# An expert's 64-token tile in a bank of the first product's ring, and two opening loads issued by other engines

## The chip, the cores and the metric

The kernel runs on one core of one Trainium2 chip. The metric is device time in microseconds (us), of which the span of a profiled execution is nearly all. The engines are TensorE (PE, its weight loads PEld), VectorE (DVE), ScalarE (ACT), GpSimd (POOL) and SyncE (SP); DMAs are issued by SP, and before the change by GpSimd only where rows are gathered or scattered.

## The reference

Three stages follow each other on 4608 tokens of 512 channels:

```python
scores = scale * np.matmul(q, k.transpose(0, 1, 3, 2))        # 8 batches, 8 heads, 576 x 64
attn = np.matmul(scores * Dmat, v)                            # decay mask gamma^(i-j), i >= j
y = (((x @ w1) * (x @ w2)) @ w3) @ w_out                      # 512 -> 1024 -> 1024 -> 512
logits = y @ w_gate                                           # 8 experts
assigned = greedy by sorted logits, 576 tokens per expert
out[mask] = np.maximum(y[mask] @ e_w1[e], 0.0) @ e_w2[e]      # for each expert e
```

The weights of the middle stage come as 64-bit floats. Products are made in single precision by three products of halves: each operand is split into a high and a low part.

## The kernel before, in words

**Opening.** The list ORDER (line 23) sets the order in which SP issues the first loads: "q0 c0 k0 v0 c1 q1 k1 w0 v1 w1 ...": queries, keys and values of 128-token tile 0, 1, 2, constants c, and pairs of weight blocks w of 1 MB. Lines 1133 to 1142 walk the list and call `att_load` (line 238), which has an argument for the issuing engine that is SP by default. q and k of a tile are two DMAs each, v is one; their pieces are 64 floats, 256 bytes (128 rows by 8 heads for a tile). Two small buffers are cleared by GpSimd behind the loads, and SP then loads the router's weights (lines 1143 to 1145).

Attention of tile 0 runs through `att_scale` (line 261, VectorE scales q and k), `att_T` (274 to 276, transposes and a ScalarE copy), `att_P` (300, the first product that reads v and k), `att_QK` (283), `att_mask` (288), `att_state` (312). Beside it, `conv` (185 to 216) turns 64-bit weights into single-precision high and low parts: one ScalarE operation (196), four on VectorE (197 to 202), a copy and a subtraction (215, 216). The first weight products are at line 549.

**Experts.** `expert(e)` (line 1014) takes 576 tokens. Its first product (line 1027) is made in two halves of 256 and 320 tokens, for 8 blocks f of the hidden channels: 12 matmuls each into a PSUM bank that goes round a ring of four, HB = PX + PYb (line 982). PX are two tiles of one bank each (p2, p3; the profile calls them p); PYb are the two banks of one tile, PY (the profile's py). ScalarE (1036) and VectorE (1037) empty each bank into the operands `ht`; the second half is emptied in two pieces, of 256 and 64 columns.

The second product (line 1049) makes five output tiles o: four of 128 tokens (24 matmuls each), and tile 4 of 64 tokens (16 matmuls, for which the high and low operands lie side by side). Each takes a bank from `mm_bank()` (line 130), which alternates between the two banks MM. A tile is emptied by ScalarE (1055), tile 4 by ScalarE and a VectorE add (1058, 1059), into `osb`, two buffers in turn (1052), and GpSimd scatters it to the output rows (1060). Experts 0 to 6 write the tiles in the order 0, 1, 2, 3, 4, expert 7 in the order 0, 4, 1, 2, 3.

The order of instructions on each engine is fixed when the program is built, from dependencies and a timeline of the builder's own; the experts' part stands in a block of its own for that (line 1166). Side by side with an expert, the next one's weights are split (940, 941) and its tokens gathered (990), transposed (1005) and split (1010, 1011).

Of the kernel before, what the change touches and what calls it, by code (L numbers as in the profile page):

```python
# [84 lines left out]
def build(ctx, tc, io):  # L85
    nc = tc.nc
    PE, V, A, G, SP = nc.tensor, nc.vector, nc.scalar, nc.gpsimd, nc.sync
# [42 lines left out]
    def mm_bank():  # L130
        return MM[nxt("mm", 2)]

    def nxt(name, n):
        i = rot[name]
        rot[name] = (i + 1) % n
        return i
# [6 lines left out]
    def slot(i, k):  # L143
        if WS[i] is None:
            WS[i] = region(f"ws{i}", 4096, F32R)
        if (i, k) not in views:
            views[i, k] = WS[i].rearrange("p (k f) -> p k f", k=k)
        return views[i, k]
# [15 lines left out]
    def load_pair(n):  # L164

        t = RO[n // 2 % 2][:, 2048 * (n % 2):2048 * (n % 2) + 2048]
        i, w = n // 2, ("w1", "w2")[n % 2]
        for x in range(2):
            raws[w, 2 * i + x, 0] = t.bitcast(I32).rearrange("p (k x f c) -> p k x f c", k=4, x=2, c=2)[:, :, x]
        SP.dma_start(t.bitcast(mybir.dt.int64).rearrange("p (k f) -> p k f", k=4),  # L170
                     w64[w].rearrange("(k p) f -> p k f", k=4)[:, :, 256 * i:256 * i + 256])
# [47 lines left out]
    qkv = [[A0[:, 1024 * j + 512 * i:1024 * j + 512 * i + 512] for j in range(3)] for i in range(2)]  # L219
# [4 lines left out]
    def buf(t):  # L224

        b = qkv[t if t < 3 else (t + 1) % 2]
        return b[0], qkv[t % 3][1], b[2]
# [10 lines left out]
    def att_load(t, which=(0, 1, 2), eng=SP):  # L238
        for i in which:
            if t >= NT or (t, i) in loaded:  # L240
                continue
            loaded.add((t, i))
            x, src = buf(t)[i], (q, k, v)[i]
            p = 0
            while p < 128:
                b, s = divmod(128 * t + p, S)
                n = min(128 - p, S - s)
                if i == 2:
                    eng.dma_start(x[p:p + n].rearrange("p (h d) -> p h d", h=H),
                                 src[b, :, s:s + n, :].rearrange("h s d -> s h d"))  # L250
                else:
                    for r in range(2):
                        eng.dma_start(x[p:p + n].rearrange("p (c r d) -> p r c d", c=4, r=2)[:, r],
                                     src[b, 4 * r:4 * r + 4, s:s + n, :].rearrange("h s d -> s h d"))
                p += n
# [715 lines left out]
    def hT():  # L971

        if not hts:
            r = [region(f"g{j}", 3072, F32R) for j in range(3)] + [region("h3", 512, F32R)]
            for f in range(6):
                b = 1152 * (f % 2)
                hts.append((r[f // 2][:, b:b + 512], r[f // 2][:, b + 512:b + 1024], r[f // 2][:, b + 1024:b + 1152]))
            hts.append((r[0][:, 2304:2816], r[1][:, 2304:2816], r[0][:, 2816:2944]))
            hts.append((r[2][:, 2304:2816], r[3][:, 0:512], r[1][:, 2816:2944]))
        return hts  # L980

    HB = PX + PYb
# [31 lines left out]
    def expert(e):  # L1014
        wh, wl = (slot(i, 4) for i in pairs[(2 * e) % 3])
        yh = [h[:, k] for _, h, _ in yts[e % 2] for k in range(h.shape[1])]
        yl = [l[:, k] for _, _, l in yts[e % 2] for k in range(l.shape[1])]
        ht = hT()
        for half in range(2):
            ts = (slice(0, 256), slice(256, 576))[half]  # L1020
            n = ts.stop - ts.start
            for f in range(8):
                fs = slice(128 * f, 128 * f + 128)
                p = HB[nxt("hb", 4)]
                for kk in range(4):
                    for j, (w, x) in enumerate(((wh, yh), (wh, yl), (wl, yh))):
                        PE.matmul(p[:, :n], w[:, kk, fs], x[kk][:, ts], start=(kk == 0 and j == 0),  # L1027
                                  stop=(kk == 3 and j == 2))
                hh, hl, hr = ht[f]
                if half:  # L1030
                    parts = ((p[:, 0:256], hh[:, 256:512], hl[:, 256:512]),
                             (p[:, 256:320], hr[:, 0:64], hr[:, 64:128]))
                else:
                    parts = ((p[:, 0:256], hh[:, 0:256], hl[:, 0:256]),)
                for src, h, l in parts:
                    A.activation(h, src, AF.Relu)  # L1036
                    V.scalar_tensor_tensor(l, src, 0.0, h.bitcast(F32), op0=OP.max, op1=OP.subtract)  # L1037
                yield 1500
        vh, vl = (slot(i, 8) for i in pairs[(2 * e + 1) % 3])
        for o in (0, 1, 2, 3, 4) if e < E - 1 else (0, 4, 1, 2, 3):  # L1040
            p = mm_bank()
            for f in range(8):
                if o < 4:
                    s = slice(128 * o, 128 * o + 128)
                    ops = ((ht[f][0][:, s], vh), (ht[f][0][:, s], vl), (ht[f][1][:, s], vh))
                else:
                    ops = ((ht[f][2], vh), (ht[f][2], vl))
                for j, (x, w) in enumerate(ops):
                    PE.matmul(p, x, w[:, f, :], start=(f == 0 and j == 0), stop=(f == 7 and j == len(ops) - 1))  # L1049
                if f % 2:  # L1050
                    yield 1300
            ob = osb[nxt("osb", 2)]
            n = 128
            if o < 4:
                A.activation(ob, p, AF.Copy)  # L1055
            else:
                n = 64
                A.activation(ob[:64], p[64:128], AF.Copy)
                V.tensor_tensor(ob[:64], p[:64], ob[:64], op=OP.add)  # L1059
            st = G.indirect_dma_start(out=out, out_offset=bass.IndirectOffsetOnAxis(ap=idx[:n, 5 * e + o:5 * e + o + 1], axis=0),  # L1060
                                      in_=ob[:n], in_offset=None)
            for x in scat:
                tc.declare_no_dep(st.ins, x.ins, reason="rows of other tokens")
            scat.append(st)
# [68 lines left out]
    for c in ORDER.split():  # L1133
        n = int(c[1:])
        if c[0] == "c":
            a, b = (0, 272, 400, CST.shape[1])[n:n + 2]
            SP.dma_start(cst[:, a:b], io["cst"][:, a:b])
        elif c[0] == "w":
            load_pair(n)
            nload[0] = n + 1  # L1140
        else:
            att_load(n, ("qkv".index(c[0]),))
    G.memset(wg, 0.0)
    SP.dma_start(wg[:, :, 0:8], io["wgate"].rearrange("(c p) e -> p c e", p=128))
    G.memset(WG, 0.0)
# [20 lines left out]
    with tc.block(schedule_with_timeline_sim=True):  # L1166
        begin = tokens(0)
        drain(take_from(begin, 2))
        for e in range(E):
            def side(e=e):  # L1170
                if e + 1 < E:
                    yield from weights(e + 1, 1, V)
                    yield from tokens(e + 1)
            s = side()
            m = expert(e)
            if e == 0:
                drain(take_from(m, 3))
                drain(begin)
                drain(take_from(m, 3))
                drain(weights(0, 1, V))  # L1180
                drain(weights(1, 0, V))
                drain(take_from(m, 10))
            else:
                drain(take_from(m, 16))
            merge(m, s, 1.2)
            drain(s)
            if e + 2 < E:
                drain(weights(e + 2, 0, V))
# [28 lines left out]
```

## Time and profile before

| | |
|---|---|
| median of 3 runs | 1303.81 us (1303.66 to 1306.4) |
| profiled execution, its own time | 1303.38 us |
| its span | 1301.6 us |
| TensorE busy | 1256.4 us, 97% |
| VectorE, ScalarE, GpSimd busy | 41%, 35%, 20% |
| mean granted TensorE clock | 0.984 of full |

The span is what the profiler saw from the first to the last instruction; the execution's own time holds 1.78 us more. Busy times are sums over instructions. A bracket behind a row of the timeline gives the idle time of the engine ahead of it and what ended it.

### The profile page before, as it was taken

The page shows a single profiled execution, that of the slowest core. Times are in us where ns is not written, and L with a number is a line of the kernel's source. Part 1 is how long each engine was busy: PE and PEld are TensorE (multiplying, and loading weights), DVE is VectorE, ACT ScalarE, POOL GpSimd, SP SyncE. Part 2 cuts the span into 40 slices and gives each one's busy share as a digit, 9 for nine tenths or more (in the row PEclk, how much of TensorE's full clock was granted, in tenths as well). Part 3 has the DMA queues.
Part 4 walks back from the last instruction along what each step waited for, and adds up shares of the span by engine and source line. Part 5 has one row for each costly group of instructions (what it writes and reads, how often), then busy time and mean ns, then how long its engine had stood idle before and what let it go on. Part 6 is the DMA issues. An engine that isn't in the chain of part 4 may idle for free. (4 is left out here: it accounts for less than half of the span.)

```text
span 1301.6 us, 27200 instructions
## 1 busy us (share of the span) xinstructions
PE 1256.4 (97%) x11416; PEld 1112.1 (85%) x11416; DVE 529.0 (41%) x1298; ACT 460.8 (35%) x989; POOL 254.4 (20%) x238
## 2 busy tenths in 40 slices
PE   5789999999999999999999999989999999999996
PEld 4678988889898989889899777778989989899885
DVE  6797544433231312212212555553533524335220
ACT  4443433343322222212221544333543534435221
POOL 1101211112211120201110734432120211211011
PEclk7799999999999999999999999999999999999999
DMA  9766444422312131424012312163533524435110
GB/s 243 221 163 198 133 131 134 127 64 61 83 34 74 25 83 25 131 87 134 10 49 93 114 45 98 42 190 119 154 121 114 157 67 150 140 96 153 47 39 29
DMA packets 156382, 136.00 MB, mean 104 GB/s; under 512 B 119264, under 2 KB 119520, under 8 KB 155232
## 3 DMA queue, kind: packets, MB, share of 16 engines
q1 hardware_dynamic: 150368, 115.35, 30.3%
q0 software_dynamic: 5888, 18.88, 4.6%
q8 instruction: 91, 1.49, 0.5%
q14 instruction: 35, 0.29, 0.1%
HBM read 107.19 MB, written 27.00 MB: 103 GB/s over the span
## 5 line engine op out<-in xcount | busy, mean ns | idle before, releaser
L549 PE MATMUL p<-x,ws 128*128 128x384 f32 x2304 | 424.1, 339 | 1.7 <-POOL x L345 0.9
L549 PEld LDWEIGHTS p<-x,ws 128*128 128x128 f32 x2304 | 398.2, 189 | 9.8 <-issue 3.9
L1049 PE MATMUL p<-ws,g 128*128 128x512 f32 x864 | 217.9, 394 | 1.9 <-DVE rs L1059 1.4
L1049 PEld LDWEIGHTS p<-ws,g 128*128 128x128 f32 x864 | 156.5, 188 | 31.6 <-DVE rs L1059 1.8
L904 PE MATMUL p<-ws,x 128*128 128x512 f32 x576 | 140.3, 398 | 0.0
L558 DVE TENSOR_TENSOR g<-p,ms 128x384 f32<-128x384 f32 x88 | 48.9, 556 | 183.1 <-PE p L549 180.2
L904 PEld LDWEIGHTS p<-ws,x 128*128 128x128 f32 x576 | 104.8, 189 | 20.6 <-issue 0.7
L941 DVE TENSOR_TENSOR ws<-x,ws 128x512 fp32r<-128x512 f32 x120 | 80.8, 690 | 100.6 <-ACT ws L940 92.7
L261 POOL TENSOR_TENSOR a<-a,cst 128x512 f32<-128x512 f32 x52 | 54.9, 1056 | 302.4 <-DMA a<-q 223.0
L940 ACT ACTIVATE ws<-x 128x512 fp32r<-128x512 f32 x128 | 78.2, 629 | 74.4 <-DMA x<-ew 57.8
L556 ACT ACTIVATE ms<-p 128x384 f32<-128x384 f32 x96 | 47.0, 489 | 151.4 <-PE p L549 149.6
L345 POOL TENSOR_TENSOR x<-a,x 128x256 fp32r<-128x256 f32 x64 | 49.4, 783 | 258.6 <-ACT x L344 258.6
L1060 POOL DMA_INDIRECT out<-rs,idx x40 | 40.0, 999 | 266.6 <-ACT g L1036 147.0
L601 PE MATMUL p<-ws,g 128*128 128x512 f32 x288 | 71.9, 398 | 0.0
L601 PEld LDWEIGHTS p<-ws,g 128*128 128x128 f32 x288 | 52.5, 188 | 13.4 <-issue 2.5
L1027 PE MATMUL p<-a,ws 128*128 128x320 f32 (+1 forms) x384 | 58.9, 301 | 0.5 <-ACT a L1010 0.5
L1036 ACT ACTIVATE g<-py 128x256 fp32r<-128x256 f32 x96 | 31.5, 328 | 75.1 <-PE py L1027 65.1
L1027 PE MATMUL p<-x,ws 128*128 128x320 f32 (+1 forms) x384 | 57.3, 297 | 0.3 <-DVE g L1037 0.3
L1027 PE MATMUL py<-a,ws 128*128 128x320 f32 (+1 forms) x384 | 57.0, 296 | 0.0
L1027 PEld LDWEIGHTS p<-a,ws 128*128 128x128 f32 x384 | 55.1, 193 | 2.1 <-ACT a L1010 0.6
L1027 PE MATMUL py<-x,ws 128*128 128x320 f32 (+1 forms) x384 | 56.4, 296 | 0.3 <-DVE g L1037 0.3
L1027 PEld LDWEIGHTS py<-x,ws 128*128 128x128 f32 x384 | 54.0, 189 | 2.6 <-DVE g L1037 0.7
(191 smaller groups left out, 1484.6 us busy)
## 6 DMA issues: line engine op xcount, KB each, us to landing
x<-ew SPq DMA_DIRECT2D x128, 256.0 KB
y_scratch<-ms SPq DMA_DIRECT2D x36, 256.0 KB
a<-k SPq DMA_DIRECT2D x64, 128.0 KB
ws<-w SPq DMA_DIRECT2D x8, 1024.0 KB
a<-q SPq DMA_DIRECT2D x62, 128.0 KB
a<-v SPq DMA_DIRECT2D x31, 256.0 KB
g_scratch<-g SPq DMA_DIRECT2D x8, 768.0 KB
g<-g_scratch SPq DMA_DIRECT2D x4, 1536.0 KB
```

The source lines that it names most:

```text
L261: (V if t < Q0 else G).tensor_tensor(xx, xx, tb_[:, :, None].to_broadcast([128, H, DH]), op=OP.mult)
L345: G.tensor_tensor(xl.rearrange("p (s a) i -> p s a i", s=2), f, xh.bitcast(F32).rearrange("p (s a) i -> p s a i", s=2), op=OP.subtract)
L549: PE.matmul(p[:, :TB], w[:, kk, fs], x[:, kk, :], start=(kk == 0 and j == 0), stop=(kk == 3 and j == 2))
L556: A.activation(a, p[:, :TB], AF.Copy)
L558: V.tensor_tensor(g[:, f, :], p[:, :TB], a, op=OP.mult)
L601: PE.matmul(p, x[:, f, ts], w[:, f, :], start=(f == 0 and j == 0), stop=(f == 7 and j == 2))
L904: PE.matmul(p, x[:, f, :], w[:, f, :], start=(f == 0 and j == 0), stop=(f == 7 and j == 2))
L940: A.activation(h, st, AF.Copy)
L941: low.tensor_tensor(lo[:, 512 * u:512 * u + 512], st, h.bitcast(F32), op=OP.subtract)
L1027: PE.matmul(p[:, :n], w[:, kk, fs], x[kk][:, ts], start=(kk == 0 and j == 0), stop=(kk == 3 and j == 2))
L1049: PE.matmul(p, x, w[:, f, :], start=(f == 0 and j == 0), stop=(f == 7 and j == len(ops) - 1))
L1060: st = G.indirect_dma_start(out=out, out_offset=bass.IndirectOffsetOnAxis(ap=idx[:n, 5 * e + o:5 * e + o + 1], axis=0), in_=ob[:n], in_off ...
```

## The change

One line gives tile 4 the next bank of the first product's ring of four in place of one of the pair MM. The other has k of tile 0 issued by ScalarE (A) and v of tile 0 by GpSimd (G); all other loads stay with SP (the rest of the line is as before).

```diff
         for o in (0, 1, 2, 3, 4) if e < E - 1 else (0, 4, 1, 2, 3):
-            p = mm_bank()
+            p = mm_bank() if o < 4 else HB[nxt("hb", 4)]
...
-            att_load(n, ("qkv".index(c[0]),))
+            att_load(n, ("qkv".index(c[0]),), A if c == "k0" else G if c == "v0" else SP)
```

## Rows read from the trace of the kernel before

**Rows 1.** Busy us by stretch: PE, PEld, DVE, ACT, POOL, PEclk, DMA share, GB/s.
```profile
0.00:25.00 25.00, 14.15 (x322) 12.13 (x322) 13.85 (x31) 8.94 (x17) 1.39 (x7) 0.84 0.92 249
25.00:50.00 25.00, 14.12 (x228) 11.38 (x227) 23.07 (x48) 11.25 (x22) 3.42 (x4) 0.50 0.66 167
...
950.00:1000.00 50.00, 50.00 (x310) 45.43 (x309) 22.32 (x49) 22.11 (x53) 9.40 (x10) 1.00 0.42 127
...
1250.00:1292.30 42.30, 40.06 (x212) 33.92 (x211) 6.08 (x17) 7.32 (x21) 3.82 (x4) 1.00 0.07 23
```
**Rows 2.** The same view in stretches of 1 us, opening.
```profile
2.00:3.00 1.00, 0.00 (x0) 0.00 (x0) 0.00 (x0) 0.04 (x1) 0.00 (x0) 1.00 0.89 201
...
4.00:5.00 1.00, 0.00 (x0) 0.00 (x0) 0.50 (x1) 0.00 (x0) 0.00 (x0) 1.00 0.78 176
```
**Rows 3.** Timeline of 0 to 25 us: start, us, engine, line, operation, tiles, count.
```profile
0.75 1.28 ACT L276 ACT_TABLE_LOAD   x1 [0.75 <-PEq L1205]
...
2.33 0.98 SPq L253 DMA_DIRECT2D a<-k  x2
3.36 0.51 SPq L249 DMA_DIRECT2D a<-v  x1
...
6.88 0.60 SPq L170 DMA_DIRECT2D ws<-w  x1
...
7.74 1.13 PE L300 MATMUL p<-a 64*64 64x64 f32 x32
7.85 1.08 ACT L276 ACTIVATE a<-p 128x512 f32<-128x512 f32 x2 [5.81 <-PE p L274]
...
14.44 1.22 ACT L196 ACTIVATE g<-ws 128x512 f32<-128x512 f32 x2 [1.57 <-DMA ws<-w]
15.13 0.43 DVE L197 TENSOR_SCALAR g<-g 128x512 f32<-128x512 f32 x1 [3.21 <-ACT g L196]
```
**Rows 4.** Timeline: the first gather on GpSimd and the first instruction that uses it.
```profile
854.31 1.15 POOL L990 DMA_INDIRECT a<-y_scratch,idx  x1 [7.49 <-DMA x<-ew]
...
858.76 0.51 PE L1005 MATMUL p<-identR,a 128*128 128x128 f32 x4 [2.63 <-DMA a<-y_scratch,idx]
```
**Rows 5.** Timeline of TensorE between two py products (expert 4), and one p run.
```profile
1102.95 1.92 PE L1027 MATMUL py<-a,ws 128*128 128x320 f32 x12
...
1104.93 4.49 PE L1049 MATMUL p<-ws,g 128*128 128x512 f32 x19
...
1109.62 0.93 PE L1049 MATMUL p<-ws,g 128*128 128x512 f32 x3
1110.38 1.93 PE L1027 MATMUL py<-a,ws 128*128 128x320 f32 x12
...
1251.92 3.69 PE L1027 MATMUL p<-x,ws 128*128 128x320 f32 x24
```
**Rows 6.** Timeline of the last 25 us (expert 7).
```profile
1271.63 1.09 PE L1049 MATMUL p<-ws,g 128*128 128x512 f32 x4
...
1273.24 2.02 PE L1027 MATMUL py<-x,ws 128*128 128x320 f32 x12 [0.29 <-DVE g L1037]
...
1284.38 0.73 PE L1049 MATMUL p<-ws,g 128*128 128x512 f32 x2
...
1286.52 5.51 PE L1049 MATMUL p<-ws,g 128*128 128x512 f32 x23 [1.40 <-DVE rs L1059]
1286.74 0.90 POOL L1060 DMA_INDIRECT out<-rs,idx  x1 [0.43 <-DVE rs L1059]
...
1291.86 0.39 PE L1049 MATMUL p<-ws,h 128*128 128x512 f32 x1
1292.29 0.60 ACT L1055 ACTIVATE rs<-p 128x512 f32<-128x512 f32 x1 [6.54 <-PE p L1049]
1293.16 0.97 POOL L1060 DMA_INDIRECT out<-rs,idx  x1 [5.52 <-ACT rs L1055]
```
**Rows 7.** Waits of 1245 to 1302 us: engine, line, releaser, us in total, times, longest.
```profile
PE p L1049 <- ACT rs L1055: 0.5, 1, 0.5
```

## The prediction

> **What bounds the kernel now.** I read the busy shares by stretch first. In the first 50 us VectorE carries the kernel: it is busy 13.85 of 25 us, then 23.07 of 25, while TensorE is busy 14 of 25. From about 140 us to the end TensorE is full, 50.00 of 50 us in the stretch shown, and only at the end do 2.24 of 42.30 us stay empty [rows 1]. So the change can act in two ways only: an earlier start of the VectorE-bound opening moves everything behind it, and at the end empty time of TensorE, or the path behind its last product, can shrink or grow. In between it counts only if it makes TensorE wait.
>
> The opening in microsecond stretches shows the DMA engines near full from 2 us on, with small holes [rows 2]. The timeline shows what VectorE waits for: its weight conversions begin at 15.13, behind ScalarE's first conversion at 14.44, which waited for the 1 MB of weights that SP issued at 6.88. VectorE had finished the masks of tile 0 at 11.92 and sat idle 3.21 us [rows 3].
>
> For the experts I read TensorE's order. First products in one-bank tiles (names p) come in runs of 24, two banks back to back; those in py, one tile of two banks, only ever come 12 at a time, with other products between them. One py product waits 0.29 us for VectorE to empty the py product just before it, which went to the other bank [rows 5, 6]. So py behaves as one unit: one product, then its eviction, then the next.
>
> The last 20 us show the end. TensorE waits 1.40 us for the add that empties the 64-token tile (4), because the one tile that is left needs its bank; then come 24 products, a ScalarE copy, and the scatter at 1293.16 [rows 6]. Another 0.50 us goes to a bank of the same pair [rows 7].
>
> **Start.** Two SP instructions for k and one for v leave SP's queue, 2.33 to 3.87; all that SP issues behind them can come 1.54 us sooner [rows 3]. They are issued on ScalarE and GpSimd, in front of ScalarE's table load (1.28 us) and of two memsets on GpSimd. ScalarE's first copy is at 7.85 after 5.81 us idle, so two issues of about 0.5 us are hidden there [rows 3]; the cleared buffers are read by the router weights' load only about 20 us in. Both cost nothing as long as those covers stand. The gain is not 1.54 us, since the weights queue behind the loads of two tiles on DMA engines that are already busy: what an earlier issue can fill is the holes, 0.11 us in 2 to 3 and 0.22 us in 4 to 5 [rows 2]. I take -0.3 us, with -1.5 as the lower end.
>
> The price of v on GpSimd is not shown. The nearest row is a gather: 128 rows, 1.15 us on GpSimd, used 4.45 us after its start [rows 4]. The load of v has 1024 pieces (128 rows by 8 heads). Begun near 0.5 us it lands between 4.9 (priced as one gather) and 13 us (eight times the 1.15, and 3.3 to land). The first product with v starts at 7.74 and the masks end 4.2 us after that, so a landing up to about 10.5 is hidden behind the wait for weights [rows 3]; at 13 it costs 2.5 us. I take 0, nearer the one gather, since a scatter of 64 rows takes 0.90 us on GpSimd [rows 6], not half the 1.15, so that rows are the small part; I keep +2.5.
>
> **Tile 4's bank.** The edit moves no arithmetic: 16 products, the copy and the add per expert stay. It moves tile 4 from the pair MM to the ring of four (PX0, PX1, and the two banks of py), and the ring then advances 17 per expert in place of 16. Tile 4 of expert e lands in ring place e mod 4: in py for experts 2, 3, 6 and 7.
>
> Removed: the two bank waits at the end, 1.40 [rows 6] and 0.50 [rows 7]; the 0.29 of the py wait may go as well. All of TensorE's idle time before its last product is 2.19, so its end could move from 1292.25 (1291.86 + 0.39, [rows 6]) to 1290.06.
>
> Added in the middle: for experts 2, 3 and 6, tile 4 becomes a ninth link in a chain of eight py products and holds both py banks, so the next expert's py products wait for its copy and add. Between two py products there stand now 22 matmuls and more at one place [rows 5], 5 (the row of 4 and a single one) at another [rows 6]; only the short gap costs, 0.29. The order is fixed when the program is built, and tile 4's 16 matmuls leave the filling for the chain. I take two short gaps at 0.29 in each of three experts, +1.7 us; ends 0 (other work covers, as in [rows 5]) and two gaps at the longest wait seen, 1.40, +8.4.
>
> Added at the end: tile 4 of expert 7 lies in py, so its products come after the eviction of the last py product, with nothing of it done earlier; I take it last, ending with TensorE at 1290.06. The order there is 0, 4, 1, 2, 3, the output buffers alternate, and so tile 2 must use the buffer that tile 4's scatter reads. In the trace this costs nothing: tile 4's scatter starts at 1286.74 and tile 2 is copied at 1292.29 [rows 6]. Now the chain is: tile 4's last matmul, 1.63 us to its scatter (1284.38 + 0.73 to 1286.74), the scatter until the buffer is free, then 0.87 from copy to last scatter (1292.29 to 1293.16) [rows 6]. The time to a free buffer is not shown: at least the 0.90 on GpSimd [rows 6], and the gather's 4.45 [rows 4] as the upper end. I take 3.5, near the gather, with half its bytes. Last scatter: 1290.06 + 1.63 + 3.5 + 0.87 = 1296.06, against 1293.16: +2.9 us, ends +0.3 and +3.9.
>
> The Trainium skill, "DMA: Bandwidth & Descriptors", section "Anatomy of one DMA — SWDGE (gpsimd) path", fits 2.0 us plus bytes by 436 GB/s, so an estimate of 2.3 us for these 128 KB; by it the end costs +1.7 and the sum 1306.5. No row here times this release.
>
> **Sum.** The profiled execution took 1303.38 (span 1301.6 and 1.78 around it); the median of the runs is 1303.81, 0.4 above it. 1303.4 - 0.3 + 1.7 + 2.9 = **1307.7 us**.
>
> **Rivals.**
> (1) The two py banks are separate, or tile 4 is finished early anyway: the waits go and nothing replaces them. TensorE ends at 1290.06 and the last scatter follows 0.91 later as now, -2.2, with the start -0.3: 1300.9. For it: the waits are there in the rows. Against it: py products never run 24 in a row, and the 0.29 wait. It decides if tile 4's last matmul comes more than 5.1 us (1.63 and 3.5) before TensorE's end. The Trainium skill, "PSUM — Partial Sum Buffer", section "PSUM bank collisions raise a hardware error", asks for guards by bank and quadrant, which would make the two banks independent and give this rival; the wait in [rows 6] speaks against its being so here.
> (2) The chain starves TensorE: two gaps per expert at 1.40 instead of 0.29, so 1303.4 - 0.3 + 8.4 + 2.9 = 1314.4. For it: the added link recurs in three experts. Against it: now only the last expert has short gaps.
> (3) It does little: DMA engines stay full with the same bytes, TensorE full until 1250, and the end trades the bank wait for an equal buffer wait: 1303.4, give or take 1.5.
>
> **How the numbers follow.** Chances: forecast 0.50, rival (1) 0.23, (2) 0.12, (3) 0.15. A measurement of this kernel can tell about 0.2%, 2.6 us: slower means over 1306.4, faster under 1301.2. The forecast's own range is 1303.4 (tail +0.3, no middle cost) to 1311.5 (v late, buffer late); 0.42 of its 0.50 lies above 1306.4. Rival (1) lies about the lower mark: 0.14 under it, 0.09 over. Rival (3) gives 0.11 same, 0.03 faster, 0.01 slower. Sums: faster 0.17, same 0.28, slower 0.55. The range goes from 1300.8, at rival (1)'s point, to 1311.5; outside remain about half of rival (1) and most of (2).
>
> **What would show it.** Right: the last ScalarE copy idles for a scatter instead of for TensorE, and starts some 4 us behind tile 4's add; tile 4's 16 matmuls of expert 7 stand after the last py product; short waits of TensorE for VectorE or ScalarE stand before py products after experts 2, 3 and 6; VectorE's first conversion moves from 15.13 to about 14.8. Wrong: tile 4 is done well before TensorE's end, or TensorE's end is followed by a scatter within 1 us (rival 1); the first product with v starts after 10.5 us (the start costs); waits at py products near 1.4 us (rival 2).

## The result and the profile after

The changed kernel takes 1323.45 us (median of 1317.88, 1322.87, 1324.04 and 1324.37), the kernel before 1303.82 beside it: a ratio of 1.0134, with a 95% interval from 1.0113 to 1.0155. It is slower, as forecast, but by 17.5 us (by the ratio; the medians lie 19.6 apart) and not by 4: the time lies above the range.

The profiled execution took 1317.88, with a span of 1316.1; it is the lowest of the four, so it explains 14.5 us (1316.1 - 1301.6). The other three have spans of 1321.1 to 1322.6 and left no trace; what they add stays open.

First TensorE's account over the experts, from the first transpose to the end of the last product, in the view of busy time by stretch: length, busy us with the number of matmuls, granted clock, DMA share, GB/s. The kernel before:

```profile
858.76:1292.25 433.49, 430.16 (x2592) 1.00 0.37 114
```

The changed kernel, the same stretch, and the one that answers to the third stretch of [rows 1] (there PE, PEld, DVE, ACT, POOL, then the clock):

```profile
856.31:1302.43 446.12, 435.13 (x2592) 0.99 0.35 110
...
950.00:1000.00 50.00, 47.81 (x298) 42.98 (x297) 22.25 (x48) 21.37 (x51) 12.09 (x12) 1.00 0.46 145
```

With the same 2592 matmuls the stretch is 12.6 us longer. TensorE's empty time rose from 3.3 us (433.49 - 430.16) to 11.0, and its busy time by 5.0. The full stretch of before, 50.00 of 50 us, has a hole of 2.2. Behind the last product the way to the end of the span grew from 9.35 (1301.6 - 1292.25) to 13.7, and in this trace the experts start 2.45 earlier: 12.6 + 4.3 - 2.45 = 14.5.

The first 324 of the 2592 matmuls, as many as one expert has, take 3.5 of the 12.6 us (56.6 against 53.1). From the 325th on (two that still run then are counted too) the kernel before and the changed one show:

```profile
911.85:1292.25 380.40, 377.90 (x2270) 1.00 0.35 107
```
```profile
912.89:1302.43 389.54, 380.38 (x2270) 1.00 0.33 105
```

So the earlier beginning is spent within the first expert, which the start alone does too (below), and what is left for the tile is 9.1 us: 6.7 more of empty time, 2.5 more of busy time. (To about 1 us: the order changed, and 101 matmuls of 512 columns lie ahead of the 325th where 89 did before.)

Where TensorE waits, in the view of waits from 845 to 1320 us (engine, operation, releaser: us in total, times, longest):

```profile
PE p L1049 <- ACT g L1036: 7.8, 7, 2.3
PE p L1005 <- DMA a<-y_scratch,idx: 2.5, 1, 2.5
PE p L1005 <- DVE a L1011: 1.4, 1, 1.4
PE p L1049 <- ACT rs L1055: 0.5, 1, 0.5
...
```

The second stands in [rows 4] as well, the third in the first expert; the shift of the ring below has it too (1.6) and loses nothing; the fourth is that of [rows 7]. The first row is new. It is not a first product that waits for a bank but a second product (L1049) that waits for ScalarE to take a first product out of PSUM (L1036): TensorE has used up the second products whose inputs are ready. The timelines of TensorE and ScalarE, put together in order of time, show one of the three long ones (start, us, engine, line, operation, [idle before <- releaser]):

```profile
1196.19 1.59 PE L1027 MATMUL py<-a,ws 128*128 128x256 f32 x12
1196.67 0.63 ACT L940 ACTIVATE ws<-x 128x512 fp32r<-128x512 f32 x1 [0.16 <-DMA x<-ew]
1197.62 1.93 PE L1027 MATMUL p<-a,ws 128*128 128x320 f32 x12
1200.28 1.20 ACT L940 ACTIVATE ws<-x 128x512 fp32r<-128x512 f32 x2 [2.98 <-DMA x<-ew]
1201.39 0.37 ACT L1036 ACTIVATE g<-py 128x256 fp32r<-128x256 f32 x1
1201.78 0.59 ACT L1058 ACTIVATE rs<-p 64x512 f32<-64x512 f32 x1
1201.81 1.19 PE L1049 MATMUL p<-ws,g 128*128 128x512 f32 x4 [2.27 <-ACT g L1036]
...
1202.84 2.58 PE L1027 MATMUL py<-a,ws 128*128 128x256 f32 x12
```

The py product was finished at 1197.78. Its eviction is queued on ScalarE behind two conversions of weights, and these wait 2.98 us for a load; so it comes at 1201.39, 3.6 us late, TensorE stands 2.27 us, and the next py product begins only at 1202.84, and slowly (2.58 us where 1.59 is usual).

The copy at 1201.78 empties tile 4 of expert 5. Its bank is ring place 1, PX1, and not py: of the three tiles that first products have, PX0, PX1 and py, one was taken here by tile 4. The other two long holes, in the same two timelines:

```profile
977.85 0.59 ACT L1058 ACTIVATE rs<-p 64x512 f32<-64x512 f32 x1 [1.03 <-DMA out<-rs,idx]
978.47 0.38 ACT L1036 ACTIVATE g<-py 128x256 fp32r<-128x256 f32 x1
...
978.91 1.19 PE L1049 MATMUL p<-ws,g 128*128 128x512 f32 x4 [2.19 <-ACT g L1036]
...
1095.41 0.59 ACT L1058 ACTIVATE rs<-py 64x512 f32<-64x512 f32 x1
...
1102.10 1.19 PE L1049 MATMUL p<-ws,g 128*128 128x512 f32 x4 [1.61 <-ACT g L1036]
```

The first stands beside tile 4 of expert 1, in PX1 again, the second behind tile 4 of expert 3, in py. Of the 7.8 us of the new row, 5.2 stand about tile 4 of experts 1, 4 and 5, which lie in PX (2.19, 0.18 + 0.56, 2.27), 1.61 behind one in py, and 0.94 in the last expert (twice 0.47).

The clock behind the hole at 1201.81 shows why the next product is slow (PE busy, clock, DMA share, GB/s):

```profile
1200.00:1205.00 5.00, 3.19 (x15) 0.81 0.60 190
1205.00:1210.00 5.00, 5.00 (x31) 0.85 0.64 193
```

After that hole part of the time is spent at the lower level (1.2 instead of 2.4 GHz): about 1.7 us lost in 10 (5 x 0.19 + 5 x 0.15). In the first expert the three stretches of 5 us from 855 to 870 have 0.83, 0.50 and 0.99, against 1.00, 0.66 and 1.00 before, about 1.7 us more; the start alone has 0.77, 0.55 and 1.00 there and is not slower, so this part is not the tile's. Together this is some 3.4 of the 5 us of added busy time; the rest is not traced to a place.

The end, against [rows 6]:

```profile
1294.77 1.92 PE L1027 MATMUL py<-x,ws 128*128 128x320 f32 x12
...
1298.64 3.79 PE L1049 MATMUL py<-ws,g 128*128 128x512 f32 x16
...
1302.46 0.59 ACT L1058 ACTIVATE rs<-py 64x512 f32<-64x512 f32 x1 [2.98 <-PE py L1049]
1303.09 0.68 DVE L1059 TENSOR_TENSOR rs<-py,rs 64x512 f32<-64x512 f32 x1 [5.01 <-ACT rs L1058]
1304.05 0.90 POOL L1060 DMA_INDIRECT out<-rs,idx  x1 [3.33 <-DVE rs L1059]
1306.73 0.60 ACT L1055 ACTIVATE rs<-p 128x512 f32<-128x512 f32 x1 [3.67 <-DMA out<-rs,idx]
1307.60 0.97 POOL L1060 DMA_INDIRECT out<-rs,idx  x1 [2.65 <-ACT rs L1055]
```

Tile 4 stands last, all 16 products behind the last first product; tile 2's copy then waits for the buffer that tile 4's scatter reads. The opening, against [rows 3]:

```profile
1.29 1.08 POOL L249 DMA_DIRECT2D a<-v  x1 [0.85 <-POOLq L1205]
...
1.86 1.28 ACT L276 ACT_TABLE_LOAD   x1 [1.86 <-issue]
...
8.61 1.13 PE L300 MATMUL p<-a 64*64 64x64 f32 x32
...
12.33 1.23 ACT L196 ACTIVATE g<-ws 128x512 f32<-128x512 f32 x2 [0.19 <-DMA ws<-w]
13.26 0.76 DVE L197 TENSOR_SCALAR g<-g 128x512 f32<-128x512 f32 x2
```

VectorE's first conversion comes at 13.26 where it came at 15.13.

### The profile page after: what moved, and what is told of

It reads as the page before. It is cut to its first block, busy times and chain, and to the rows that moved or that the text cites. A ratio compares the mean times of both kernels' runs of the same rounds, so it can differ in the third digit from the quotient of the medians.

```text
span 1316.1 us, 27178 instructions
## 1 busy us (share of the span) xinstructions
PE 1260.6 (96%) x11416; PEld 1114.8 (85%) x11416; DVE 529.1 (40%) x1298; ACT 458.6 (35%) x989; POOL 256.1 (19%) x239
## 5 line engine op out<-in xcount | busy, mean ns | idle before, releaser
L1049 PE MATMUL p<-ws,g 128*128 128x512 f32 x800 | 207.7, 396 | 8.7 <-ACT g L1036 7.8
L1049 PEld LDWEIGHTS p<-ws,g 128*128 128x128 f32 x800 | 143.6, 189 | 36.2 <-ACT g L1036 10.5
L1037 DVE SCALAR_TENSOR_TENSOR g<-py,g 128x256 fp32r<-128x256 f32 (+1 forms) x88 | 30.8, 350 | 102.6 <-ACT g L1036 102.6
L601 PE MATMUL p<-ws,g 128*128 128x512 f32 x288 | 71.9, 398 | 0.0
L1036 ACT ACTIVATE g<-py 128x256 fp32r<-128x256 f32 x96 | 31.5, 328 | 115.6 <-PE py L1027 104.9
L601 PEld LDWEIGHTS p<-ws,g 128*128 128x128 f32 x288 | 52.5, 188 | 13.3 <-issue 2.5
L1027 PEld LDWEIGHTS py<-a,ws 128*128 128x128 f32 x384 | 55.9, 195 | 2.0
```

The lines of the kernel that those rows point to most:

```text
L601: PE.matmul(p, x[:, f, ts], w[:, f, :], start=(f == 0 and j == 0), stop=(f == 7 and j == 2))
```

## The experiments

The first question was which half of the change costs the time, the second why py does. Line numbers in a trace shift by one to three where an edit adds lines.

**The start alone** (e1_start_only). Of the change only the issue of k and v:

```diff
-            att_load(n, ("qkv".index(c[0]),))
+            att_load(n, ("qkv".index(c[0]),), A if c == "k0" else G if c == "v0" else SP)
```

> Only the two opening loads are moved; tile 4 keeps its bank of the pair. If the loss comes from tile 4's bank alone, this kernel keeps the earlier opening that the changed kernel's profile shows (its experts begin 2.3 us sooner) and nothing else: 1301.5 us, 0.2% faster than before. If the moved loads cost something further on (the longer times of the unprofiled runs, say), it is at or above 1304.

Measured: 1303.38, ratio 0.9991 [0.9981, 1.0001]. No difference that can be told; the 1301.5 of the first case did not come. TensorE's order of matmuls in the experts is that of before, and from the 325th on the time is the same:

```profile
911.92:1292.35 380.43, 378.17 (x2270) 1.00 0.34 107
```

The experts begin at 857.02, 1.74 earlier than before, and the 325th matmul starts at 911.92 against 911.85: what the beginning gains in this trace is lost in the first expert.

**The bank alone** (e2_bank_only):

```diff
-            p = mm_bank()
+            p = mm_bank() if o < 4 else HB[nxt("hb", 4)]
```

> Only tile 4 takes the ring's bank; all loads are issued by SP. If the two parts add up, this is the changed kernel plus the 2.3 us that the opening gained: about 1320 us in the profiled run and 1326 in the median. If the parts act together (the opening shifts the experts' loads into a worse place), it is clearly below the changed kernel's 1323.

Measured: 1319.09, ratio 1.0115 [1.0098, 1.0132], with the waits of the whole change (6.1 us in 7 times for ScalarE's L1036). This half carries the loss. It lies 4.4 below the whole change, but the two intervals overlap: whether the two moved loads add to the loss is not shown. Its experts begin at 856.57, as early as those of the whole change at 856.31 though its opening is that of before; over all traces of this study the beginning lies between 855.83 and 859.62, and no earlier with k and v moved than without, so the 2.45 us above are not shown to be the start's gain.

**The changed kernel with py as two tiles** (e6_split_py):

```diff
-    PY = ps.tile([128, 1024], F32, name="py")
-    PYb = [PY[:, 512 * i:512 * i + 512] for i in range(2)]
+    PYb = [ps.tile([128, 512], F32, name=f"py{i}") for i in range(2)]
...
-        A.activation(ft[:, :, n], PY.rearrange("p (s b) -> p s b", s=2)[:, :, 256 + n.start:256 + n.stop], AF.Copy)
+        for s in range(2):
+            A.activation(ft[:, s, n], PYb[s][:, 256 + n.start:256 + n.stop], AF.Copy)
```

> The changed kernel with py made of two tiles of one bank each in place of one tile of two (one ScalarE copy of the attention becomes two smaller ones, for 36 tiles). If py acts as one unit and this is the cause, first products can alternate over four banks, tile 4 blocks one bank only, and the time falls below the kernel before: 1300 us or less. If the cause is the shifted ring or the waits for DMAs in ScalarE's queue, it stays above 1315.

Measured: 1301.07, ratio 0.9975 [0.9965, 0.9985]: faster than before; 1300 or less was expected. The row of L1036 is gone, and what the waits from 845 to 1320 us still list for banks of first products is

```profile
PE py L1027 <- DVE g L1037: 0.2, 1, 0.2
PE p L1027 <- DVE g L1037: 0.2, 1, 0.2
```

The same banks and the same ring, with TensorE's order built anew: the loss hangs on py being one tile.

**A third output buffer for the last tile 4** (e7_third_buffer). The changed kernel, with tile 4 of the last expert in a free staging buffer:

```diff
             ob = osb[nxt("osb", 2)]
+            if e == E - 1 and o == 4:
+                ob = xs[0][:, 0:512]
```

> The changed kernel, with a third output buffer for expert 7's tile 4 (the idle staging buffer of the weights). The order of TensorE is the changed kernel's. If the last copy waits for tile 4's scatter to free its buffer, that wait (3.67 us idle on ScalarE) goes, and the end is tile 4's own copy, add and scatter: about 3.5 us less than the changed kernel. If the wait is for something else, nothing changes.

Measured: 1315.73, ratio 1.0081 [1.0064, 1.0098], 3.4 us below the bank alone (1319.09) beside which it ran. Its end in the timeline:

```profile
1301.39 3.79 PE L1049 MATMUL py<-ws,g 128*128 128x512 f32 x16
...
1303.51 0.97 POOL L1062 DMA_INDIRECT out<-rs,idx  x1 [0.30 <-issue]
1305.21 0.59 ACT L1060 ACTIVATE x<-py 64x512 f32<-64x512 f32 x1 [2.77 <-PE py L1049]
1305.84 0.68 DVE L1061 TENSOR_TENSOR x<-py,x 64x512 f32<-64x512 f32 x1 [5.01 <-ACT x L1060]
1306.80 0.90 POOL L1062 DMA_INDIRECT out<-x,idx  x1 [2.32 <-DVE x L1061]
```

Tile 2 is copied and scattered before tile 4, and the last scatter starts 1.62 us behind the last product (1305.18) where it was 5.17 (1307.60 - 1302.43). So the buffer is the loss at the end, and the greater part is elsewhere.

**Tile 4 in PX** (e3_tile4_px), one bank of its own each time, start and ring as before:

```diff
-            p = mm_bank()
+            p = mm_bank() if o < 4 else PX[e % 2]
```

> Before, with tile 4 of expert e in PX[e mod 2], a tile of one bank; the ring still advances 16 per expert, and the start is as before. Theory A (the loss comes from the two banks of py being one unit, so that the ninth link in its chain waits for an eviction in ScalarE's queue): PX banks have no partner, so the middle costs nothing, TensorE's waits at p L1049 behind ScalarE g L1036 stay under 1 us in sum, and the waits of 1.40 and 0.50 us for MM banks at the end go: 1300.5 to 1304. Theory B (it is enough that tile 4 takes a bank of the ring, whichever it is, because the first products then have a bank less for a while): waits behind ScalarE g L1036 as in the bank hunk alone (some 6 us), and 1312 or more.

Measured: 1315.13, ratio 1.0083 [1.0059, 1.0106]. Theory A missed, and theory B's time was hit, but not by B's waits:

```profile
PE p L1027 <- DVE g L1037: 3.4, 3, 1.7
PE py L1027 <- DVE g L1037: 2.8, 3, 1.2
...
PE p L1049 <- ACT g L1036: 1.5, 4, 0.5
```

Here first products themselves wait for a bank. Its end has the same buffer wait, last product 1299.75 and last scatter 1305.17, 5.42 behind it, 4.5 us more than before; the experts' stretch is 442.2 us, 8.7 more than before, 5.2 of them from the 325th matmul on (385.6 against 380.4). So a tile in PX is not free either, and the 12.6 of the whole change belong to four tiles in PX and three in py ahead of the last. (In the whole change three ring places lie between a tile 4 and the next first product in its bank, here none or one, so a tile in PX need not cost the same in both.) The theory was narrowed to this one (U): what counts is how many units are emptied independently. With py as one tile the ring's four banks are three units, PX0, PX1 and py; tile 4 leaves two of them to the next expert's first products. With py split there are four, and three stay.

**The ring's shift alone** (e4_shift_only). Tile 4 stays in MM, and the ring moves on as in the change:

```diff
             p = mm_bank()
+            if o == 4:
+                nxt("hb", 4)
```

> Before, with tile 4 in MM as it was, but the ring of four advanced by one more place where tile 4 comes, so that the blocks f of each expert fall on the banks that they have in the changed kernel. Theory A (tile 4 as a ninth py product is the cause): py has eight products per expert as before, so 1302 to 1306 and TensorE's waits behind ScalarE g L1036 under 1.5 us in sum. Theory B (the shift of the ring alone does it, by where py products fall against the halves and the loads of weights): 1312 or more, with the waits of the bank hunk alone.

Measured: 1303.59, ratio 0.9996 [0.9986, 1.0007]. The shift costs nothing.

**Tile 4 of every expert in py** (e5_tile4_py):

```diff
-            p = mm_bank()
+            p = mm_bank() if o < 4 else PYb[e % 2]
```

> Before, with tile 4 of every expert in py, bank e mod 2; the ring still advances 16. Theory A (each tile 4 in py costs some waits of TensorE in the middle): seven experts in the middle have the ninth link where the bank hunk alone had three, the end is the same as there. The bank hunk alone lost about 15 us, of which about 4 stand at the end and 11 in the middle, so 7/3 of 11 and 4: about 1304 + 26 + 4 = 1334, range 1322 to 1345. Rival (the loss belongs to a few single moments at which ScalarE's queue stands at a load, not to the number of tiles in py): within 5 us of the bank hunk alone, 1314 to 1324.

Measured: 1331.65, ratio 1.0217 [1.0191, 1.0242]. This is within theory A's range, and the rival, a few single moments, is out. The experts' stretch is 25.1 us longer than before (458.6 against 433.5) with seven tiles in py ahead of the last, 8.7 with seven in PX. From the 325th matmul on it is 23.5 (403.9 against 380.4) and 5.2: 3.4 and 0.7 us for each, so a tile in py is the dearer. But the expectation lays the whole loss of the bank alone to its three tiles in py; with four in PX beside them these prices would give some 13 (an estimate, 3 x 3.4 + 4 x 0.7), and 9.1 was measured in the whole change.

**The kernel before with py split** (e8_before_split): the diff of e6_split_py on the kernel before, tile 4 in MM.

> Before, with py made of two tiles of one bank each (the copy of the attention's output in two pieces), tile 4 in MM. It asks how much of the 2.5 us by which the changed kernel with split py beat the kernel before is the split alone. If the split does it by itself (TensorE's waits for py go): 1300 to 1302. If it was tile 4 leaving MM (the waits of 1.40 and 0.50 us at the end): 1303 to 1305, with both waits still there.

Measured: 1299.53, ratio 0.9962 [0.9951, 0.9973]. The split does it by itself: the experts' stretch is 430.9 us against 433.5, and the waits of 1.40 and 0.50 us at the end [rows 6, 7] are gone although tile 4 is still in MM. Tile 4 in the ring then brings nothing that can be told (e6_split_py is not faster).

**A ring of three banks, two ways** (e9_ring_px_px_py and e10_ring_px_py_py), tile 4 in MM, py one tile:

```diff
-    HB = PX + PYb
+    HB = PX + PYb[:1]
...
-                p = HB[nxt("hb", 4)]
+                p = HB[nxt("hb", 3)]
```

and for the second `HB = PX[:1] + PYb`.

> Before, with the first products' ring cut from four banks to three: PX0, PX1 and one bank of py; tile 4 stays in MM. Theory U (what counts is how many units there are that are emptied independently; py with two banks is one unit): still three units, and py carries 5.3 products per expert instead of 8, so nothing is lost: 1299 to 1305. Theory B (what counts is the number of banks for first products): one bank less all the time, where tile 4 in PX took one for a part of the time and cost 11 us: 1312 or more.

> Before, with the ring cut to three banks in the other way: PX0 and both banks of py; tile 4 stays in MM. Theory U: two units instead of three, all the time, and py carries 10.7 products per expert instead of 8: a loss larger than that of tile 4 in PX, 1320 to 1400. Theory B: the same time as with PX0, PX1 and one bank of py, within 5 us.

Measured: 1300.44, ratio 0.9972 [0.9962, 0.9981], and 1332.25, ratio 1.0216 [1.0197, 1.0235]. With the same number of banks one is faster than before, the other 28 us slower. TensorE's waits in the first, all four rows:

```profile
PE p L1005 <- DMA a<-y_scratch,idx: 2.3, 1, 2.3
PE p L1005 <- issue: 2.0, 1, 2.0
PE p L1027 <- ACT a L1010: 0.5, 1, 0.5
PE p L1027 <- DVE h L1037: 0.4, 1, 0.4
```

and in the second the row that the change brought, much grown:

```profile
PE p L1049 <- ACT g L1036: 14.7, 27, 1.1
```

Giving a bank of py away gains time, as theory U has it: the bank was no unit of its own. The first ring also gives py fewer products (5.3 per expert for 8), and the second more (10.7), so that a shorter chain in py alone would explain these two runs as well; it does not explain the loss with tile 4 in PX, where py keeps its eight.

**Split and start together** (e11_split_and_start): e8_before_split with the diff of e1_start_only.

> Before with py as two tiles of one bank, and k and v of tile 0 issued by ScalarE and GpSimd as in the change; tile 4 stays in MM. With py split alone 1299.5 was measured. If the 1.5 to 2.3 us that the opening gained in the traces reach the end when no wait is left in the experts: 1297 to 1298.5. If they are lost at the first expert, as with the start alone: 1299 to 1300.5.

Measured: 1300.91, ratio 0.9976 [0.9966, 0.9986]. Near the second figure, a little above it: the start gains nothing even where TensorE waits for no bank and no eviction in the experts.

**Shorter weight loads** (e12_quarter_loads), on the changed kernel. It leaves out three quarters of the rows of each load of weights, from the third expert on:

```diff
+            nr = 128 if e < 2 else 32
...
-                SP.dma_start(st, src[128 * u:128 * u + 128, :])
+                SP.dma_start(st[:nr], src[128 * u:128 * u + nr, :])
```

and the same in the load of the other matrix.

> The changed kernel, with 32 rows instead of 128 in each load of expert weights from the third expert on (so its output is computed from partly stale weights); all conversions and products stay. Theory Q (the loss in the middle comes from evictions that stand in ScalarE's queue behind conversions that wait for loads): these waits go, and of some 10 us in the middle under 4 are left: 1308 to 1315. Theory C (the chain of products in py is too long with a ninth link, whatever ScalarE waits for): the loss stays, 1317 to 1324.

Measured: 1312.37, ratio 1.0063 [1.0047, 1.0080]. ScalarE's wait for loads and TensorE's for evictions (the lines are one higher here):

```profile
ACT ws L941 <- DMA x<-ew: 26.0, 34, 3.2
```

```profile
PE p L1050 <- ACT g L1037: 1.9, 6, 0.5
```

against these waits of ScalarE in the changed kernel:

```profile
ACT ws L940 <- DMA x<-ew: 49.1, 52, 3.6
...
ACT rs L1055 <- DMA out<-rs,idx: 6.6, 2, 3.7
```

The experts' stretch is 438.2 us, so 7.9 of the 12.6 us are gone; the buffer wait at the end stays. From the 325th matmul on it takes

```profile
916.10:1297.32 381.22, 378.44 (x2270) 1.00 0.18 58
```

against 389.54 in the changed kernel, whose first 324 matmuls are the same, and 380.40 before: 8.3 of the 9.1 us behind the first expert are gone. That speaks for theory Q, with a reservation: the builder orders the instructions anew for each kernel, and here too the order of the experts changed (from the 395th matmul), so that the two effects are not cleanly apart. Loads alone don't do it either: the kernel before waits 53.5 us for them on ScalarE (the same row of its waits), and TensorE waits there for no eviction before a second product.

The same reservation holds for the study as a whole. By line, tile name and shape, TensorE's order in the changed kernel is that of before only for the first 228 of the 2592 matmuls of the experts; the bank alone and the third buffer have exactly the changed kernel's order. No run moves tile 4 with the order held, so how much of the loss lies in the order that was built, and how much in the waits within it, is not shown.

The lowest time of the study is that of e8_before_split, 1299.53 us, 5.0 below the kernel before beside it (1304.55) and below the changed kernel: py as two tiles, and neither half of the change. The ring with one bank of py is not told apart from it (0.9972 against 0.9962, the intervals overlap).

## Why the prediction was right and wrong

**Start, -0.3: of the right size.** Alone it cannot be told from nothing. The weights did come earlier (VectorE's first conversion at 13.26, where about 14.8 was forecast), but no trace carries that past the first expert. The cover of v held: its issue took 1.08 us of GpSimd, near the one gather that was taken as its price, and the first product with v started at 8.61, later than the 7.74 of before but ahead of the 10.5 up to which it is hidden.

**Removed, 2.19 us of empty time: wrong.** The 1.40 is gone, the 0.50 stands, and two waits of 0.47 for evictions are new in the last expert. That the two bank waits hang on py and not on MM's two banks was not seen: with py split they are gone with tile 4 still in MM. It may be that the first products came too late and the bank was only the last link; no run shows that by itself.

**Middle, +1.7: the step that failed.** That py is one unit was right: with py split the loss is gone. But only tile 4 in py was priced, as a ninth link of its chain in experts 2, 3 and 6, at "two short gaps at 0.29 in each of three experts" with +8.4 as the upper end; tile 4 in PX, in experts 0, 1, 4 and 5, was put at nothing without a reason. The stretch grew by 12.6 us, 9.1 of them behind the first expert, and 5.2 of the 7.8 us that TensorE waits for evictions before second products stand about tiles 4 in PX. With tile 4 in PX alone the stretch grows by 8.7, 5.2 of them behind the first expert (e3_tile4_px): by theory U any bank of the ring that it takes leaves the next expert two units of three. Three more things were left out.
- The 0.29 us was a wait in a place where ScalarE was free. Where its queue stands behind conversions that wait for loads, an eviction comes 3.6 us late, as at 1201.39. In the kernel before this happened as often (for 15 of the 64 py products the eviction began more than 1 us behind the product, for 12 in the changed kernel), hidden by second products that lay ready; the prediction priced the gap by the wait that was left, not by the slack that hid the others.
- The waits show up before second products, not before py products where they were looked for: a late chain first eats the filling.
- After the hole at 1201.81 the clock was lower for some microseconds, about 1.7 us; the busy time of the same matmuls grew by 5.0 us, half of it in the first expert.

Rival (2), that the chain starves TensorE, comes nearest: TensorE ran dry behind late evictions, but before second products, and mostly at tiles in PX, which the rival does not price. Its 1314.4 lies 9 us below the median, and 3.5 below the traced execution. Its 0.12 was too little: against it stood only that short gaps are rare now, which says nothing of how much slack is left.

**End, +2.9: right in mechanism and nearly in size.** Tile 4's 16 products stand last, and tile 2 waits for its buffer. From the last product to the last scatter 6.0 us was forecast (1.63 + 3.5 + 0.87), 5.17 measured: 1.62, then 2.68 from the scatter's start to ScalarE's copy (1304.05 to 1306.73), then 0.87. The 2.68 lies between the estimate of 2.3 from the Trainium skill, "DMA: Bandwidth & Descriptors", section "Anatomy of one DMA — SWDGE (gpsimd) path", and the 3.5 that was taken, nearer the estimate. Against the end of TensorE's work the way grew by 4.3.

**Rival (1), 1300.9,** is the kernel with py split: 1301.07, its last product ended at 1289.81 and its last scatter 0.96 behind that, where 1290.06 and 0.91 were forecast. Its condition, that the two py banks are separate, was the right one to ask for, and it does not hold in the kernel as written. The Trainium skill, "PSUM — Partial Sum Buffer", section "PSUM bank collisions raise a hardware error", asks for guards by bank and quadrant. The runs show that this program waits by tile: the same two banks cost or don't as they are allocated as one tile or two.

**Sum.** In the places that the traces measure, the forecast was -0.3 for the beginning, -0.5 for the experts' stretch (-2.19 + 1.7) and +5.1 behind TensorE's last product (6.0 - 0.91), 4.3 in all on 1303.4. Measured were -2.45 (which the bank alone shows too), +12.6 and +4.3: 1317.9 for the traced execution. The second term is the miss, by 13 us, or by some 10 when the first expert's 3.5 us, in which the earlier beginning is spent, are left aside.

## What to carry to other kernels

Count the units that are freed independently, not the banks: a tile of two banks that is used half by half is one unit, and giving one half away can be faster than using both. When a chain gets a link, price it by the slack that hides its delays now (how much ready work the busy engine has, and what else stands in the queue of the engine that evicts), since the waits that are visible before are only those that the slack did not hold. Price it for every bank that it can take. And look at which tile comes last: an output buffer whose scatter still read it cost 3.67 us of ScalarE's time there, with nothing left to hide it.

## What the runs showed of the hardware

- A buffer of 64 rows read by a scatter was free 2.68 us after GpSimd began the scatter, 1.78 after the 0.90 that GpSimd worked on it.
- A plain load of 1024 pieces, issued by GpSimd, held it for 1.08 us, about as long as a gather of 128 rows (1.15, [rows 4]).
- After a hole of 2.27 us in TensorE's work the granted clock was 0.81 and 0.85 in the next two stretches of 5 us; after the hole of 2.19 us at 978.91 it stayed at 1.00 in this trace.
- The first transpose of the experts moved by 2.9 us between traces (855.83 to 858.76) of kernels whose opening is that of before: a shift of 2 us there, read from one trace, shows nothing.
